# Loading halves of K, Q and V as pairs in an attention and token-mixing kernel

## The chip, the cores and the metric

The kernel runs on one core of one Trainium2 chip. The metric is the device time of one execution in microseconds (us). Five things work side by side: TensorE (PE, with its weight loads PEld), VectorE (DVE), ScalarE (ACT), GpSimd (POOL), and 16 DMA engines, for which in this kernel SyncE (SP) issues every transfer.

## The reference

Batch 8, 8 heads, sequence 576, head width 64. The first stage is a linear attention; the second mixes the tokens of each batch and ends in a 512 x 512 projection.

```python
r_q, r_k = maximum(q, 0), maximum(k, 0)          # per position: times cos and sin
q_p = concat(r_q * cos, r_q * sin); k_p = concat(r_k * cos, r_k * sin)
kv  = einsum('bhsf,bhsd->bhfd', k_p, v); z = sum(k_p, axis=s)
x   = (q_p @ kv) / (q_p @ z + 1e-6)              # heads side by side: [8, 576, 512]
W   = einsum('bsd,btd->bst', x @ w_q, x @ w_k) / 8
out = maximum(einsum('bst,btd->bsd', W, x), 0) @ w_out
```

The inputs q, k and v have 9.4 MB each in float32, the output has 9.4 MB.

## The kernel before

**Tiling.** The work of the first stage is cut into 16 half-batches H = 0 to 15: batch H // 2, four of its heads. A half-batch has two head pairs, called a (0) and b (1). A head pair of one input is 128 partitions x 576 float32, 288 KB, each partition one contiguous run of 2304 bytes. The text calls it a quarter, since four of them make one input of one batch. It lies in half of a buffer `raw[nm][H % 5]` (five buffers for each of k, q and v).

**The order is written out by hand.** `ORDER` is one long text of words, and a loop at the end (line 555 on) turns each word into instructions. Each engine has its own queue and does its words in the order in which they stand; across engines the framework sets semaphores where one instruction needs what another made. A word has a kind, a number, perhaps a or b for one head pair alone, `@A`, `@V` or `@G` for ACT, DVE or POOL, and `:n` for the bank of PSUM. The kinds that matter here:

- LQ, LK, LV: load quarters (line 145); LW0 to LW5: load w_q, w_k and four slices of w_out; ST: store one tile of the output (line 519). All go through SP's queue.
- RQ, RK: relu and cast of q, k (ACT line 203, else line 205). CV: cast of v (lines 209 to 213), VS: v times the table of cos and sin on DVE (line 234). VG: both in one on POOL, straight from the loaded v (line 248).
- QT, KV, N (lines 295 or 301, 275 or 285, 340): transposes of q, k-times-v sums, and numerators with denominators, on PE. QM, KE, EP, RC, X (line 393) evict and divide.
- XT or XR with XE, WK, WQ, KX, MX (line 489) with ME (lines 500, 502), WO (line 509) with OE (lines 209, 213): the second stage.

**SP's queue.** SP issues loads and stores in the order of the words. The framework gives the transfers eight semaphores in turn (DMAHW0 to DMAHW7), and a transfer waits until the one eight before it has landed. A load also waits until the engines have read what was in its buffer, five half-batches earlier; a store waits for its OE.

**Before the change** the words LQ0b and LQ0a, say, stand for two transfers; a word without a or b gave two transfers as well, by the loop in `load`.

Of the kernel before, what the change touches and what calls it, by code (L numbers as in the profile page):

```python
# [23 lines left out]


ORDER = """
LQ1a LV1b LQ1b LV1a LK1b LK1a LV0a LV0b LQ0b LQ0a LK0a LK0b LV3b LK3a LV3a LQ3b LQ3a LK3b LQ2a LW0
LV2a LV2b LW1 LK2a LQ2b LK2b TK TV CV1b@A TI T2 TZ CV1a@A TQ RQ1@G TB TW QT1:0 RK1b@V CV0@G LV5a
RQ0b@A VS1b RK1a@V VS1a KV1:6 KE1@A QM1 VS0 RQ0a@V RK0@A LK5a LV5b LK5b LQ5a LQ5b LQ4a LQ4b LV4a
LV4b LK4a LK4b RQ3a@A N2:2 N3:6 QT0:0 EP3@V EP2@V KV0:4 RJ1 X2 QM0 WU9:2 KE0@V VG3a WU6:0 N1:0 X3  # L30
EP1@V RQ3b@A N0:4 VG3b RK3@A XT1:2 RQ2a@G QT3:6 CV2a@G EP0@V RJ0 X1 XE1@A X0 QM3 KV3:0 XT0:4 KE3@A
N6:0 CW1@A EP6@A XE0@V VG2b LV7b LV7a CW0@A WK0:6 RC6 N7:2 WQ0:7 X6 RK2a@A VG5a KW0@A RQ5@G RQ2b@A
LQ7b LK7a LQ7a VS2a EP7@A RK2b@A LK7b LQ6a LQ6b LV6b LK6b LV6a LW4 LK6a LW2 LQ8b LW3 LV8a LW5 LV8b
LQ8a RC7 KX0:1 QW0@V QT2:4 X7 XK0@A KV2:0 XT3:2 RK5a@A KE2@A QM2 RK5b@A N5:6 N4:0 CV5b@V XA0@V VS5b
EP4@A EP5@A RC5 RQ4b@G RC4 KV5:4 X5 XE3@A MX0:2 X4 CV4a@G LV9a RQ4a@A LQ9a LQ9b LK8a XB0@G ME0@A
QT5:6 CV4b@G LV9b LK8b KE5@A XR2:2 QT4:0 MX2:4 QM5 N11:6 XE2@A ME2@A WK1:2 RK4a@G EP11@A KW1@A QM4
MX1:4 VS4 ME1@A RK4b@A LK9b LK9a N10:0 KX1:2 WQ1:3 CV7a@A KV4:4 EP10@V XK1@A RJ5 QW1@A XA1@A MX5:2
KE4@A VG7b X10 X11 ME5@A RQ7a@A MX4:0 VS7a ME4@A N9:6 RC9 XT5:4 RQ7b@G N8:2 XB1@V XE5@A RQ6@A X9
EP8@V RC8 RK7@G VG6b LV11b VG6a LV11a LQ11b LQ10b LQ11a LQ10a QT7:0 KV7:6 KE7@A X8 XT4:2 MX6:4 QM7
CW3@G CW2@G QT6:6 MX7:0 ME6@A XE4@V QM6 ME7@A N15:4 WK2:2 CV8a@G N14:0 MX3:6 RK6@A LK11b LK11a CW5@G  # L40
EP14@V EP15@V ME3@A WQ2:3 KV6:6 KW2@V RC14 RC15 VG8b KE6@A CW4@A QW2@V KX2:2 X14 N13:0 N12:6 X15
RK8a@G EP12@V XR7:4 WO8:3 XK2@A WO1:2 EP13@A XA2@A XE7@A WO7:5 OE8:0@A RQ8a@A OE1:4@A RJ6 VG9b X12
X13 WO2:4 RK9a@G RQ8b@A XR6:2 XB2@G CV9a@V MX8:0 OE2:2@A VS9a RQ9@A VS8a ME8@V OE7:1@A RK8b@A QT8:6
XE6@V RK9b@A WO6:4 QT9:0 QM8 WO4:3 OE6:3@A QM9 WK3:2 KW3@A KV8:6 KV9:4 MX9:0 OE4:5@A ST4 LV10b LV10a
LQ13b LQ12b LQ13a LK10a KE8@V MX11:2 N16:6 KE9@A ME11@A ME9@A WQ3:4 EP16@V KX3:5 MX10:2 RC16 X16
XK3@V QW3@A N19:0 VG11 ME10@A N18:6 EP18@V N17:4 WO11:2 RC17 EP19@A RK11b@G RC18 RC19 RK11a@G
RQ10a@G VG10 X19 WO5:3 RQ11@A X17 RQ10b@A OE11:6@A ST11 LQ12a LV12a LK10b LK12b LV13a LV12b LQ14b
LK12a LV15b LV13b LK13b LQ14a LK14a QT11:0 X18 WO9:2 XA3@A KV11:4 QT10:6 OE5:5@A OE9:7@A KE11@A QM11
XR8:2 RQ13@G XB3@A XE8@A XR9:0 WO10:4 WO0:5 QM10 N22:6 OE10:8@A EP22@A MX13:2 RQ12a@G RQ12b@G
OE0:6@A XE9@V ME13@V MX12:0 WO12:4 RC22 X22 ME12@A WK4:5 MX15:2 N23:0 KW4@A ME15@V EP23@A MX14:6  # L50
WQ4:5 KX4:2 ME14@A RC23 WO3:3 X23 RK10@A XK4@V XB4@V QW4@A XA4@A KV10:6 OE3:9@A QT13:0 QM13
OE12:10@A ST12 LV14a LK13a LV14b LK15a WO14:5 KE10@A VG12 MX16:2 XR11:6 XE11@V OE14:11@A ME16@A
RK12@A N20:0 N21:4 WO13:2 RC21 RC20 X21 QT12:6 MX18:4 X20 WO17:3 KV12:0 QM12 ME18@A MX19:4 OE13:10@A
ST13 LQ15b XR10:6 WO16:2 RQ14a@A KE12@A RQ14b@A ME19@A OE17:13@V ST17 LQ15a LK14b XE10@V VG13 MX17:6
N24:4 OE16:12@V N25:0 ME17@A RK13a@A RK13b@A QT14:2 EP24@V QM14 EP25@V WO21:7 WK5:6 RJ12 KW5@A
OE21:10@A ST21 LK15b ST8 ST3 LV15a KV13:2 KE13@A VG14 KX5:6 X24 X25 WQ5:7 N27:2 XR12:0 RK14a@A QW5@V
N26:4 EP27@V XE12@V XK5@A XB5@A WO20:6 EP26@A RK14b@A RJ13 XA5@G X27 RQ15b@G WO19:0 KV14:2 OE20:14@A
ST20 ST0 ST7 VG15b X26 MX23:6 OE19:15@A MX21:4 WO15:1 ME23@V KE14@A XR13:2 MX20:6 ME21@A VG15a
MX22:4 OE15:17@V XE13@V WO18:0 RQ15a@A N28:2 RK15b@A ME22@A ME20@A OE18:16@V ST18 ST16 ST14 ST10
ST19 ST15 N29:4 EP29@V EP28@V RK15a@A QT15:6 RJ14 WK6:0 X28 KW6@A WO25:1 KV15:2 WQ6:0 KE15@A X29  # L60
KX6:4 OE25:13@A ST25 ST6 ST2 ST5 ST1 QM15 XR14:2 N30:6 EP30@V RC30 QW6@A N31:0 XK6@A XE14@A WO23:4
X30 EP31@A RC31 XB6@V WO26:2 X31 OE23:12@A WO24:4 XR15:6 XA6@G OE26:10@V ST26 OE24:8@A MX27:2 MX24:0
ME27@A XE15@V WO22:5 WK7:2 ME24@A OE22:0@V ST22 ST23 ST9 ST24 KW7@A MX25:0 MX26:6 WQ7:4 KX7:2 ME25@A
XK7@A XA7@G ME26@V QW7@V XB7@A WO27:3 OE27:5@A ST27 WO29:2 MX28:0 ME28@A MX29:4 MX31:6 WO30:3
OE30:12@V ST30 ME29@A MX30:0 ME31@A WO28:4 ME30@A OE29:11@A ST29 WO32:5 WO33:2 OE32:9@A ST32
OE28:4@V ST28 OE33:8@V ST33 WO34:3 WO35:4 WO31:5 OE34:5@V ST34 OE35:0@V ST35 OE31:2@A ST31
"""


# [1 line left out]
def kernel(  # L71
# [10 lines left out]
    nc = tc.nc  # L82
# [18 lines left out]
    NRAW, NPREP, NV2, NQM, NX, NXT, NOUT = (5, 2, 2, 2, 2, 2, 18)  # L101
# [12 lines left out]
    def bufs(n, shape, dtype, name):  # L114
        return [pool.tile(shape, dtype, name=f"{name}{i}") for i in range(n)]

    raw = {nm: bufs(NRAW, [P, 2, HC], FP32, f"{nm}raw") for nm in "kqv"}
# [18 lines left out]
    def srcs(src):  # L136
        return [src[b].flatten().rearrange("(pr p e) -> p pr e", pr=NPAIR, p=P)
                for b in range(B)]

    src = {"k": srcs(k), "q": srcs(q), "v": srcs(v)}  # L140

    def load(nm, H, part):
        b, h = divmod(H, 2)
        for r in (0, 1) if part is None else (part,):
            nc.sync.dma_start(raw[nm][H % NRAW][:, r, :], src[nm][b][:, 2 * h + r, :])  # L145

    coef = math.pi / 2.0 / S
    ki = pool.tile([P, C, 2], I32, name="ki")
# [49 lines left out]
    A, V, G = nc.scalar, nc.vector, nc.gpsimd  # L198
# [356 lines left out]
    for word in ORDER.split():  # L555
        word, _, eng = word.partition("@")
        word, _, ps = word.partition(":")
        part = {"a": 0, "b": 1}.get(word[-1])
        word = word.rstrip("ab")
        kind = word[:2] if word[:2] in steps or word[:2] in halves or word[0] in "LT" else word[0]  # L560
        i, ps = int(word[len(kind):] or 0), int(ps or 0)
        if kind in ("LK", "LQ", "LV"):
            load(kind[1].lower(), i, part)
        elif kind in halves:
            halves[kind](i, ps, ENG.get(eng), slice(0, 2) if part is None else
                         slice(part, part + 1))
        else:
            steps[kind](i, ps, ENG.get(eng))
# [30 lines left out]
```

## Time and profile before

| | |
|---|---|
| time, median of 3 runs | 117.84 us (117.74 to 118.74) |
| profiled execution, its own time | 116.59 us |
| its span, first to last instruction | 114.8 us |
| TensorE clock granted | 0.996 |
| PE busy / PEld | 98.0 us / 65.9 us |
| DVE / ACT / POOL busy | 87.0 / 84.1 / 73.7 us |
| DMA packets on SP's queue | 20640, 39.07 MB, 93.0% of 16 engines' span |
| loads of q, k, v | 32 each, 288 KB, 5.8 to 5.9 us from issue to landing (median) |
| stores | 36, 256 KB, 3.6 us |

How to read it: times in the views of the trace count from the start of the span. The profiled execution's own time is 1.8 us more than its span, which is what lies before and after the program's instructions. A line with "x4" stands for four instructions in a row that are merged. A bracket at a row's end says how long the engine sat idle before it and what ended that. An issue on SP (SPq) is the instruction that starts a transfer, not the transfer.

### The profile page before, as it was taken

What the parts mean: (1) busy time and instruction counts of PE and PEld (TensorE: products, weight loads), DVE (VectorE), ACT (ScalarE), POOL (GpSimd) and SP (SyncE); (2) the same over time, 40 slices, a digit from 0 to 9 for tenths busy, and PEclk for the clock granted to TensorE, in tenths of its full rate; (3) what the DMA queues carried; (4) which work ended last, traced back from release to release, by engine and by line L of the source; (5) the groups of instructions that cost most, each with busy time, mean ns of one, the idle gap of its engine ahead of it and who ended that gap; (6) DMA issues with size and microseconds to landing.
All of it is one profiled execution on the core that took longest, in us unless ns stands there. A gap on an engine that the chain in (4) does not pass through costs nothing.

```text
span 114.8 us, 4994 instructions
## 1 busy us (share of the span) xinstructions
PE 98.0 (85%) x2126; PEld 65.9 (57%) x2126; DVE 87.0 (76%) x159; ACT 84.1 (73%) x154; POOL 73.7 (64%) x62
## 2 busy tenths in 40 slices
PE   0034897897988998999999999999999999999970
PEld 0034666785776876646875566655774666563420
DVE  2039997899899998799679967798887896751450
ACT  7553419588999986999799959969678849568520
POOL 7434069965889799959699994999999901010000
PEclk9999999999999999999999999999999999999998
DMA  3999999999999999999999999999879579886494
GB/s 105 308 361 407 398 388 333 384 388 391 390 391 389 391 390 389 390 394 388 386 394 400 383 380 369 393 329 328 292 258 335 202 266 371 336 338 257 186 373 175
DMA packets 20662, 39.38 MB, mean 343 GB/s; under 512 B 3232, under 2 KB 3232, under 8 KB 20640
## 3 DMA queue, kind: packets, MB, share of 16 engines
q1 hardware_dynamic: 20640, 39.07, 93.0%
q8 instruction: 16, 0.26, 1.0%
q14 instruction: 6, 0.05, 0.1%
HBM read 29.62 MB, written 9.44 MB: 340 GB/s over the span
## 4 chain that ended last, share of the span: by engine, by line
PE 55%; DMA 16%; DVE 11%; ACT 6%; POOL 6%; SPq 2%; issue 2%; POOLq 0%; ACTq 0%; DVEq 0%
PE ps L509 26%; DMA vraw<-in_v_dram 10%; DMA wkf<-in_moe_w_k_dram 6%; PE ps L340 6%; PE ps L285 5%; POOL v L248 4%; DVE x L393 4%; PE ps L439 3%; PE ps L489 3%; PE ps L466 3%; PE ps L452 3%; PE ps L419 2%; SPq L145 2%; DVE v L234 1%; PE ps L295 1%
## 5 line engine op out<-in xcount | busy, mean ns | idle before, releaser
L248 POOL TENSOR_TENSOR v<-vraw,vtab 128x1152 bf16<-128x1152 f32 (+1 forms) x16 | 49.6, 3111 | 9.3 <-DMA vraw<-in_v_dram 5.6
L509 PE MATMUL ps<-wow,mix 128*128 128x512 bf16 x144 | 34.9, 380 | 0.0
L393 DVE TENSOR_TENSOR x<-ps,rec 128x640 bf16<-128x640 f32 x32 | 25.3, 820 | 0.7
L509 PEld LDWEIGHTS <-mix 128*128 128x128 bf16 x144 | 12.4, 98 | 14.1 <-issue 1.6
L209 ACT COPY o<-ps 128x512 f32<-128x512 f32 x25 | 14.6, 588 | 5.9 <-PE ps L509 5.4
L500 ACT ACTIVATE mix<-ps 128x576 bf16<-128x576 f32 x27 | 16.9, 651 | 1.8 <-PE ps L489 1.8
L203 ACT ACTIVATE rk<-kraw 128x576 bf16<-128x576 f32 (+1 forms) x18 | 14.4, 814 | 1.9 <-DMA kraw<-in_k_dram 1.8
L316 DVE TENSOR_TENSOR qm<-ps,qtab 128x1152 bf16<-128x1152 bf16 x22 | 15.4, 748 | 0.3 <-PE ps L295 0.3
L340 PE MATMUL ps<-kvs,qm 64*128 64x65 bf16 x640 | 14.7, 196 | 0.9 <-ACT kvs L209 0.8
L340 PEld LDWEIGHTS <-qm 64*128 64x128 bf16 x640 | 13.0, 98 | 3.8 <-issue 2.9
L295 PE MATMUL ps<-ident,rq 128*128 128x128 bf16 x99 | 8.3, 236 | 7.8 <-POOL rq L205 7.3
L203 ACT ACTIVATE rq<-qraw 128x576 bf16<-128x576 f32 (+1 forms) x15 | 11.5, 784 | 4.7 <-DMA qraw<-in_q_dram 4.6
L213 DVE COPY o<-ps 128x512 f32<-128x512 f32 x11 | 7.6, 689 | 6.2 <-ACT mix L500 3.3
L285 PE MATMUL ps<-v,rk 64*64 64x130 bf16 x432 | 9.9, 234 | 2.5 <-DVE v L234 1.4
L295 PEld LDWEIGHTS <-rq 128*128 128x128 bf16 x99 | 6.6, 106 | 9.2 <-POOL rq L205 7.6
L205 POOL TENSOR_SCALAR rq<-qraw 128x576 bf16<-128x576 f32 (+1 forms) x10 | 8.5, 860 | 3.9 <-DMA qraw<-in_q_dram 3.4
L285 PEld LDWEIGHTS <-rk 64*64 64x64 bf16 x432 | 7.9, 115 | 5.5 <-issue 1.0
L211 POOL TENSOR_SCALAR kx<-kx 64x256 bf16<-64x256 bf16 x5 | 2.0, 402 | 11.1 <-ACT kx L209 10.8
L209 ACT CAST kvs<-ps 128x260 bf16<-128x260 f32 (+1 forms) x14 | 6.2, 441 | 4.0 <-PE ps L285 3.7
L489 PE MATMUL ps<-wq,kx 64*128 64x288 bf16 x64 | 8.1, 287 | 0.4 <-POOL kx L211 0.3
L234 DVE TENSOR_TENSOR v<-vb,vtab 128x1152 bf16<-128x1152 bf16 (+1 forms) x9 | 8.4, 937 | 0.1
L209 ACT COPY xT<-ps 128x1280 bf16<-128x1280 bf16 (+1 forms) x7 | 8.2, 1178 | 0.1
(66 smaller groups left out, 132.3 us busy)
## 6 DMA issues: line engine op xcount, KB each, us to landing
qraw<-in_q_dram SPq DMA_DIRECT2D x32, 288.0 KB, 5.9
vraw<-in_v_dram SPq DMA_DIRECT2D x32, 288.0 KB, 5.8
kraw<-in_k_dram SPq DMA_DIRECT2D x32, 288.0 KB, 5.9
out_dram<-o SPq DMA_DIRECT2D x36, 256.0 KB, 3.6
wof<-in_moe_w_out_dram SPq DMA_DIRECT2D x4, 256.0 KB, 6.0
wqf<-in_moe_w_q_dram SPq DMA_DIRECT2D x1, 128.0 KB, 6.8
wkf<-in_moe_w_k_dram SPq DMA_DIRECT2D x1, 128.0 KB, 6.6
```

What stands on the lines that cost most here:

```text
L203: A.activation(dst, s, AF.Relu)
L209: A.copy(dst, s)
L234: V.tensor_mul(v2_b[H % NV2][:, part, :, :, 0:D], vb_b[H % NPREP][:, part].unsqueeze(3).to_broadcast([P, n, C, 2, D]), vtab.unsqueeze(1).t ...
L248: G.tensor_mul(dst[:, part, :, :, 0:D], s[:, part].unsqueeze(3).to_broadcast([P, n, C, 2, D]), vtab.unsqueeze(1).to_broadcast([P, n, C, 2, ...
L285: nc.tensor.matmul(kv_v[o, r, :], rk_of(H)[a, pr, c, :], v2_b[H % NV2][a, pr, c, :, 0:D + 1], start=(c == 0), stop=(c == C - 1))
L295: nc.tensor.transpose(qt_v[:, c, :], rq_b[H % NPREP][:, c, :, :], ident)
L316: V.tensor_mul(qm_b[H % NQM][:, :, r, 0:C, :], q_t[:, r].unsqueeze(1).to_broadcast([P, 2, C, H2]), qtab)
L340: nc.tensor.matmul(nv[:, pr, u, :], qm_b[H % NQM][a, s, r, 2 * u:2 * u + 2, :], kv_b[H % 2][a, r, pr if H in KV_WIDE else 0, s, 0:D + 1], ...
L393: V.tensor_tensor(x_b[b % NX][:, :, 4 * h:4 * h + 4, :].rearrange("p u (w r) d -> p r w u d", r=2)[:, r], nv[:, :, :, 0:D], rec(g).to_broa ...
L489: nc.tensor.matmul(pair(ps)[:, t, :].bitcast(FP32)[:, 0:HS], kx_b[b % 2][a, (m // 2) ^ t, (m % 2) * P:(m % 2 + 1) * P], wq_b[b % 2][a, :], ...
L500: A.activation(dst, s, AF.Relu, scale=scale_moe)
L509: nc.tensor.matmul(o, mix_b[bp % 2][:, m, rt * P:(rt + 1) * P], wow[:, m, :], start=(m == 0), stop=(m == NDM - 1))
```

## The change

Twenty-three pairs of words become one word each, and `load` makes of such a word one transfer of 128 x 2 x 576 float32 (576 KB) in place of two. In the DRAM the two runs of a partition lie 288 KB apart, in the buffer side by side. Where the two words of a pair did not stand next to each other, one was moved. Beside that some other words change places: LW0 goes behind LV2b, LW5 ahead of LV8a, LQ12b ahead of LQ13, LV15a from behind ST3 to ahead of LK13a; CW2 goes ahead of CW3 on POOL, WK2 ahead of N15 on PE, and RK11b and RK11a become one instruction on POOL.

```diff
 LQ1a LV1b LQ1b LV1a LK1b LK1a
-LV0a LV0b LQ0b LQ0a LK0a LK0b LV3b LK3a LV3a LQ3b LQ3a LK3b LQ2a LW0 LV2a LV2b LW1 LK2a
+LV0 LQ0b LQ0a LK0 LV3b LV3a LQ3b LQ3a LK3 LQ2a LV2a LV2b LW0 LW1 LK2a
...
     def load(nm, H, part):
         b, h = divmod(H, 2)
-        for r in (0, 1) if part is None else (part,):
-            nc.sync.dma_start(raw[nm][H % NRAW][:, r, :], src[nm][b][:, 2 * h + r, :])
+        r = slice(0, 2) if part is None else slice(part, part + 1)
+        nc.sync.dma_start(raw[nm][H % NRAW][:, r, :],
+                          src[nm][b][:, 2 * h + r.start:2 * h + r.stop, :])
```

The pairs, in the order of the words: LV0, LK0, LK3, LQ5, LK4, LV7, LQ7, LK7, LQ6, LK6, LQ8, LQ9, LV11, LQ11, LQ10, LK11, LV10, LQ13, LK12, LV12, LQ14, LV13, LV14.

Three places in the queues. First SP, from the loads of half-batch 4 to those of 6. The name ends in the number of the buffer and a number of the framework: kraw4 holds k of half-batch 4, vraw2, qraw2 and kraw2 hold half-batch 7, qraw1, vraw1 and kraw1 half-batch 6. Before:

```order
L145 DMA kraw4_67<-in_k_dram 128x576 x2
L145 DMA vraw2_75<-in_v_dram 128x576 x2
L145 DMA qraw2_70<-in_q_dram 128x576
L145 DMA kraw2_65<-in_k_dram 128x576
L145 DMA qraw2_70<-in_q_dram 128x576
L145 DMA kraw2_65<-in_k_dram 128x576
L145 DMA qraw1_69<-in_q_dram 128x576 x2
L145 DMA vraw1_74<-in_v_dram 128x576
L145 DMA kraw1_64<-in_k_dram 128x576
L145 DMA vraw1_74<-in_v_dram 128x576
L527 DMA wof_133<-in_moe_w_out_dram 128x512
L145 DMA kraw1_64<-in_k_dram 128x576
```

The same place after the change:

```order
L144 DMA kraw4_67<-in_k_dram 128x2x576
L144 DMA vraw2_75<-in_v_dram 128x2x576
L144 DMA qraw2_70<-in_q_dram 128x2x576
L144 DMA kraw2_65<-in_k_dram 128x2x576
L144 DMA qraw1_69<-in_q_dram 128x2x576
L144 DMA vraw1_74<-in_v_dram 128x576 x2
L527 DMA wof_133<-in_moe_w_out_dram 128x512
L144 DMA kraw1_64<-in_k_dram 128x2x576
```

Fourteen transfers became nine. LQ7a now comes ahead of LK7a, and LK6b behind LV6a and LW4. The bytes ahead of LV6b (the first vraw1) are the same.

Second, SP between the stores ST12 and ST13 (both from buffer o10): vraw4 is v of half-batch 14, kraw3 k of 13, kraw0 k of 15, vraw0 v of 15. One piece of the difference:

```order
-L145 DMA vraw4_77<-in_v_dram 128x576
-L145 DMA kraw3_66<-in_k_dram 128x576
-L145 DMA vraw4_77<-in_v_dram 128x576
-L145 DMA kraw0_63<-in_k_dram 128x576
+L144 DMA vraw0_73<-in_v_dram 128x576
+L144 DMA kraw3_66<-in_k_dram 128x576
+L144 DMA vraw4_77<-in_v_dram 128x2x576
+L144 DMA kraw0_63<-in_k_dram 128x576
```

LV15a came in ahead of LK13a, and LV14 is whole and stands where its second half stood.

Third, POOL at the relu of k of half-batch 11 (buffer kraw1 to rk1), the one place where POOL's rows differ (the exchange of CW2 and CW3 does not show, since both read and write the same tile):

```order
 L248 TENSOR_TENSOR v21_85<-vraw1_74,vtab_127 128x36x64
-L205 TENSOR_SCALAR rk1_79<-kraw1_64 128x576 x2
+L205 TENSOR_SCALAR rk1_79<-kraw1_64 128x1152
 L205 TENSOR_SCALAR rq0_80<-qraw0_68 128x9x64
 L248 TENSOR_TENSOR v20_84<-vraw0_73,vtab_127 128x36x64
```

Two instructions became one of twice the width; nothing else moved there.

More of the change, by code (lines that the diff above doesn't have):

```diff
@@ L26 @@
 ORDER = """
[L27 to L66, printed above, removed]
+LQ1a LV1b LQ1b LV1a LK1b LK1a LV0 LQ0b LQ0a LK0 LV3b LV3a LQ3b LQ3a LK3 LQ2a LV2a LV2b LW0 LW1 LK2a
@@ new lines @@
+LQ2b LK2b TK TV CV1b@A TI T2 TZ CV1a@A TQ RQ1@G TB TW QT1:0 RK1b@V CV0@G LV5a RQ0b@A VS1b RK1a@V
+VS1a KV1:6 KE1@A QM1 VS0 RQ0a@V RK0@A LK5a LV5b LK5b LQ5 LQ4a LQ4b LV4a LV4b LK4 RQ3a@A N2:2 N3:6
+QT0:0 EP3@V EP2@V KV0:4 RJ1 X2 QM0 WU9:2 KE0@V VG3a WU6:0 N1:0 X3 EP1@V RQ3b@A N0:4 VG3b RK3@A XT1:2
+RQ2a@G QT3:6 CV2a@G EP0@V RJ0 X1 XE1@A X0 QM3 KV3:0 XT0:4 KE3@A N6:0 CW1@A EP6@A XE0@V VG2b LV7
+CW0@A WK0:6 RC6 N7:2 WQ0:7 X6 RK2a@A VG5a KW0@A RQ5@G RQ2b@A LQ7 VS2a EP7@A RK2b@A LK7 LQ6 LV6b LV6a
+LW4 LK6 LW2 LW3 LW5 LV8a LV8b LQ8 RC7 KX0:1 QW0@V QT2:4 X7 XK0@A KV2:0 XT3:2 RK5a@A KE2@A QM2 RK5b@A
@@ new lines @@
+N5:6 N4:0 CV5b@V XA0@V VS5b EP4@A EP5@A RC5 RQ4b@G RC4 KV5:4 X5 XE3@A MX0:2 X4 CV4a@G LV9a RQ4a@A
+LQ9 LK8a XB0@G ME0@A QT5:6 CV4b@G LV9b LK8b KE5@A XR2:2 QT4:0 MX2:4 QM5 N11:6 XE2@A ME2@A WK1:2
+RK4a@G EP11@A KW1@A QM4 MX1:4 VS4 ME1@A RK4b@A LK9b LK9a N10:0 KX1:2 WQ1:3 CV7a@A KV4:4 EP10@V XK1@A
+RJ5 QW1@A XA1@A MX5:2 KE4@A VG7b X10 X11 ME5@A RQ7a@A MX4:0 VS7a ME4@A N9:6 RC9 XT5:4 RQ7b@G N8:2
+XB1@V XE5@A RQ6@A X9 EP8@V RC8 RK7@G VG6b VG6a LV11 LQ11 LQ10 QT7:0 KV7:6 KE7@A X8 XT4:2 CW2@G MX6:4
+QM7 CW3@G QT6:6 MX7:0 ME6@A XE4@V WK2:2 QM6 ME7@A N15:4 CV8a@G N14:0 MX3:6 RK6@A LK11 CW5@G WQ2:3
@@ new lines @@
+EP14@V EP15@V ME3@A KV6:6 KW2@V RC14 RC15 VG8b KE6@A CW4@A QW2@V KX2:2 X14 N13:0 N12:6 X15 RK8a@G
+EP12@V XR7:4 WO8:3 XK2@A WO1:2 EP13@A XA2@A XE7@A WO7:5 OE8:0@A RQ8a@A OE1:4@A RJ6 VG9b X12 X13
+WO2:4 RK9a@G RQ8b@A XR6:2 XB2@G CV9a@V MX8:0 OE2:2@A VS9a RQ9@A VS8a ME8@V OE7:1@A RK8b@A QT8:6
+XE6@V RK9b@A WO6:4 QT9:0 QM8 WO4:3 OE6:3@A QM9 WK3:2 KW3@A KV8:6 KV9:4 MX9:0 OE4:5@A ST4 LV10 LQ12b
+LQ13 LK10a KE8@V MX11:2 N16:6 KE9@A ME11@A ME9@A WQ3:4 EP16@V KX3:5 MX10:2 RC16 X16 XK3@V QW3@A
+N19:0 VG11 ME10@A N18:6 EP18@V N17:4 WO11:2 RC17 EP19@A RC18 RC19 RK11@G RQ10a@G VG10 X19 WO5:3
@@ new lines @@
+RQ11@A X17 RQ10b@A OE11:6@A ST11 LQ12a LK10b LK12 LV12 LQ14 LV13 LV15b LK13b LK14a QT11:0 X18 WO9:2
+XA3@A KV11:4 QT10:6 OE5:5@A OE9:7@A KE11@A QM11 XR8:2 RQ13@G XB3@A XE8@A XR9:0 WO10:4 WO0:5 QM10
+N22:6 OE10:8@A EP22@A MX13:2 RQ12a@G RQ12b@G OE0:6@A XE9@V ME13@V MX12:0 WO12:4 RC22 X22 ME12@A
+WK4:5 MX15:2 N23:0 KW4@A ME15@V EP23@A MX14:6 WQ4:5 KX4:2 ME14@A RC23 WO3:3 X23 RK10@A XK4@V XB4@V
+QW4@A XA4@A KV10:6 OE3:9@A QT13:0 QM13 OE12:10@A ST12 LV15a LK13a LV14 LK15a WO14:5 KE10@A VG12
+MX16:2 XR11:6 XE11@V OE14:11@A ME16@A RK12@A N20:0 N21:4 WO13:2 RC21 RC20 X21 QT12:6 MX18:4 X20
@@ new lines @@
+WO17:3 KV12:0 QM12 ME18@A MX19:4 OE13:10@A ST13 LQ15b XR10:6 WO16:2 RQ14a@A KE12@A RQ14b@A ME19@A
+OE17:13@V ST17 LQ15a LK14b XE10@V VG13 MX17:6 N24:4 OE16:12@V N25:0 ME17@A RK13a@A RK13b@A QT14:2
+EP24@V QM14 EP25@V WO21:7 WK5:6 RJ12 KW5@A OE21:10@A ST21 LK15b ST8 ST3 KV13:2 KE13@A VG14 KX5:6 X24
+X25 WQ5:7 N27:2 XR12:0 RK14a@A QW5@V N26:4 EP27@V XE12@V XK5@A XB5@A WO20:6 EP26@A RK14b@A RJ13
+XA5@G X27 RQ15b@G WO19:0 KV14:2 OE20:14@A ST20 ST0 ST7 VG15b X26 MX23:6 OE19:15@A MX21:4 WO15:1
+ME23@V KE14@A XR13:2 MX20:6 ME21@A VG15a MX22:4 OE15:17@V XE13@V WO18:0 RQ15a@A N28:2 RK15b@A ME22@A
@@ new lines @@
+ME20@A OE18:16@V ST18 ST16 ST14 ST10 ST19 ST15 N29:4 EP29@V EP28@V RK15a@A QT15:6 RJ14 WK6:0 X28
+KW6@A WO25:1 KV15:2 WQ6:0 KE15@A X29 KX6:4 OE25:13@A ST25 ST6 ST2 ST5 ST1 QM15 XR14:2 N30:6 EP30@V
+RC30 QW6@A N31:0 XK6@A XE14@A WO23:4 X30 EP31@A RC31 XB6@V WO26:2 X31 OE23:12@A WO24:4 XR15:6 XA6@G
+OE26:10@V ST26 OE24:8@A MX27:2 MX24:0 ME27@A XE15@V WO22:5 WK7:2 ME24@A OE22:0@V ST22 ST23 ST9 ST24
+KW7@A MX25:0 MX26:6 WQ7:4 KX7:2 ME25@A XK7@A XA7@G ME26@V QW7@V XB7@A WO27:3 OE27:5@A ST27 WO29:2
+MX28:0 ME28@A MX29:4 MX31:6 WO30:3 OE30:12@V ST30 ME29@A MX30:0 ME31@A WO28:4 ME30@A OE29:11@A ST29
@@ L67 @@
+WO32:5 WO33:2 OE32:9@A ST32 OE28:4@V ST28 OE33:8@V ST33 WO34:3 WO35:4 WO31:5 OE34:5@V ST34 OE35:0@V
+ST35 OE31:2@A ST31
 """
```

## The prediction

> **What bounds the kernel now.** I read the slices of the page first, then the stages, then the chain of waits, then the queues around the place where the chain changes its engine. The slices (40 of 2.87 us each) of PE and of the DMA engines:
>
> ```profile
> PE   0034897897988998999999999999999999999970
> DMA  3999999999999999999999999999879579886494
> GB/s 105 308 361 407 398 388 333 384 388 391 390 391 389 391 390 389 390 394 388 386 394 400 383 380 369 393 329 328 292 258 335 202 266 371 336 338 257 186 373 175
> ```
>
> From the second slice to the 26th or so the DMA engines are full, at 388 to 394 GB/s in most slices; from the 17th on PE is full. Where one takes over from the other is seen in two stages (busy us by engine, then clock, DMA share, GB/s):
>
> ```profile
> 8.00:45.20 37.20, 31.66 (x727) 25.25 (x727) 34.62 (x66) 27.95 (x48) 26.23 (x18) 1.00 1.06 387
> 45.20:111.20 66.00, 65.69 (x1399) 40.02 (x1398) 51.18 (x88) 50.94 (x98) 42.88 (x26) 1.00 0.92 337
> ```
>
> In the 66.00 us after 45.20 PE is busy for 65.69: it has 0.31 us to give back. Before that it sits idle for 5.54 of 37.20 us. The chain (start, us, what) says what holds it there:
>
> ```profile
> 9.13 5.99 DMA vraw<-in_v_dram
> 15.13 0.02 issue
> 15.14 6.64 DMA wkf<-in_moe_w_k_dram
> ...
> 40.42 4.71 POOL v L248 x2
> 45.13 0.04 issue
> 45.17 0.72 PE ps L285 x36
> ...
> 105.82 5.30 PE ps L509 x24
> ```
>
> First loads, then evictions, then POOL's two VG instructions of half-batch 6, then at 45.17 the 36 matmuls of KV6, and from there on nearly nothing but PE. So the end is the start of KV6 plus about 66 us of PE work plus the 3.6 us of last store. **Only what moves KV6, or makes PE wait after it, moves the time.**
>
> The middle rows also show how SP works: a load issued at 9.13 landed at 15.13, and at 15.14 the transfer eight places behind it went out. In the full stretch an issue therefore tells, less 0.02, when the transfer eight before it landed. The issues on SP (start, us, how long the issue took):
>
> ```profile
> 33.10 0.33 SPq L145 DMA_DIRECT2D qraw<-in_q_dram  x1
> 33.86 0.33 SPq L145 DMA_DIRECT2D vraw<-in_v_dram  x1
> 34.59 0.33 SPq L145 DMA_DIRECT2D kraw<-in_k_dram  x1
> 35.35 0.33 SPq L145 DMA_DIRECT2D vraw<-in_v_dram  x1
> ...
> 40.26 0.33 SPq L145 DMA_DIRECT2D vraw<-in_v_dram  x1
> ```
>
> These are LQ6b, LV6b, LK6b, LV6a and LV8a, so LK4b landed at 33.08, LV7b at 33.84, LV7a at 34.57, LQ7b at 35.33 and LV6b at 40.24. A quarter lands every 0.75 us. POOL and DVE at that place:
>
> ```profile
> 33.02 0.67 POOL L205 TENSOR_SCALAR rk<-kraw 128x576 bf16<-128x576 f32 x1
> 34.00 3.12 POOL L248 TENSOR_TENSOR v<-vraw,vtab 128x1152 bf16<-128x1152 f32 x1 [0.32 <-DMA vraw<-in_v_dram]
> 37.10 1.17 POOL L205 TENSOR_SCALAR rq<-qraw 128x576 bf16<-128x576 f32 x1
> 38.23 1.15 POOL L205 TENSOR_SCALAR rk<-kraw 128x1152 bf16<-128x1152 f32 x1
> 40.40 4.71 POOL L248 TENSOR_TENSOR v<-vraw,vtab 128x1152 bf16<-128x1152 f32 x2 [1.02 <-DVE x L393]
> 33.44 1.45 DVE L234 TENSOR_TENSOR v<-vb,vtab 128x2304 bf16<-128x2304 bf16 x1
> 36.86 0.88 DVE L234 TENSOR_TENSOR v<-vb,vtab 128x1152 bf16<-128x1152 bf16 x1
> ```
>
> They are RK4a, VG7b, RQ7b, RK7, then VG6b with VG6a; on DVE VS4 and VS7a. VG7b starts 0.16 after its load landed, and so does VG6b (40.24 to 40.40; the DVE instruction named in its bracket writes x, which VG6b does not read, and ends at 40.41, so I take the load). KV6 thus hangs on the landing of LV6b: plus 0.16, plus 4.71, is 45.11. If that came earlier, ACT's ME3 is next, since it empties the bank for KV6:
>
> ```profile
> 43.20 1.16 ACT L203 ACTIVATE rk<-kraw 128x1152 bf16<-128x1152 f32 x1
> 44.27 0.63 ACT L500 ACTIVATE mix<-ps 128x576 bf16<-128x576 f32 x1
> ```
>
> It ends at 44.90, so KV6 can gain about 0.2 us before something else is late.
>
> **The change part by part.** *Fewer transfers.* The bytes ahead of LV6b are the same; nine pairs (LV0 to LQ6) stand ahead of it. What a boundary between two transfers costs the engines no row shows. From above: a quarter at 390 GB/s takes 0.756 us, at 407, the best full slice, 0.725, so at most 0.03. From below: nothing. The GB/s row does not fall in slices 13 to 16 (389 to 391), where the shorter transfers of w_out bring more boundaries, so I take 0.01. Nine times that is **-0.09 us** on KV6, bounds 0 and -0.27, the latter cut to -0.2 by ME3.
>
> *A first half waits for its second.* In a pair the second half lands when it did, the first one quarter or more later. Sixteen of the 23 are read by one instruction already, which waited for both: nothing. Of the seven others, LQ8, LQ10, LQ14 and LK11 are read behind KV6, where PE sets the pace; with LQ8 and LQ14 the half that is read first landed second in any case. LQ7 stands one place earlier, so lands near 36.0, against 37.10 for RQ7b: nothing. Two remain. RK4a now waits for LK4b, 33.08 + 0.16 = 33.24 in place of 33.02: +0.2, and VS4 behind it on DVE as much. VG7b waits for LV7a: 34.57 less 0.06 for six boundaries, plus 0.16, is 34.67 in place of 34.00: +0.67. Queued behind it on POOL are RQ7b and RK7; PE waits for them with QT7 and KV7:
>
> ```profile
> 39.02 0.66 PE L295 MATMUL ps<-ident,rq 128*128 128x128 bf16 x9
> 39.61 1.19 PE L275 MATMUL ps<-v,rk 64*128 64x260 bf16 x18
> 45.17 0.72 PE L285 MATMUL ps<-v,rk 64*64 64x130 bf16 x36 [0.38 <-POOL v L248]
> ```
>
> If all 0.67 went through, RK7 would end at 40.05 in place of 39.38 and KV7 start some 0.48 late. PE idles 0.38 before KV6, of which 0.22 are free of ME3 (44.95 against 45.17), so KV6 would be 0.26 late. But VG7b took 3.12 where each of VG6 took 2.36: 0.76 were lost, and VS4 ran until 34.89. RQ7b took 1.17 against 0.67 for RK4a, and VS7a ran until 37.74. Twice an instruction on POOL that began under a VS ended as if it had begun 0.14 before that VS ended (37.12 - 2.36 = 34.76; 38.27 - 0.67 = 37.60). By these rows the 0.67 fall into a time that VG7b loses anyway, and only the 0.2 by which RK4a pushes VS4 are left: RK7 ends near 39.6, KV7 starts at 39.6. **0 us**, bounds 0 and +0.26.
>
> The Trainium skill, SBUF — State Buffer, section "Who interferes with whom", says so as a rule: DVE with two inputs in SBUF and a POOL instruction that reads SBUF take a shared port in turns, and the later one is blocked altogether. By it the sum is 0 here; were it a slowdown that travels with the instruction, it would be +0.26. The trace agrees with the rule, with the two differences above.
>
> VG6b itself is not reached: RK7 ends at 39.4 to 40.05, VG6b waits for its load until 40.3.
>
> *Exchanges.* LV3a, LQ3b, LQ3a and LV2 land 0.7 earlier, but ACT's CW1 still waits for wkf, with the same bytes ahead of it: 0. LW0 lands 1.5 later, before wkf: 0. LK6b moves behind LV6a; RK6 waits for LK6a, as before, and ACT has no idle time before it (its row at 43.20 has no bracket): 0. WK2 goes ahead of N15 on PE, to 42.43, and needs XE4 from DVE:
>
> ```profile
> 41.65 0.75 DVE L213 COPY xT<-ps 128x1152 bf16<-128x1152 bf16 x1
> 42.43 0.49 PE L340 MATMUL ps<-kvs,qm 64*128 64x65 bf16 x20
> ```
>
> XE4 ends at 42.40, just in time: 0; should it come 0.2 late with VS4, PE waits 0.2, which the 0.22 before ME3 cover. RK11 whole takes 1.15 (as RK7) for two of 0.67 on POOL, which does not hold the chain by then: 0.
>
> *Late loads.* LV15a comes forward past ST13, ST17, ST21, ST8 and ST3, and LV14 lands up to a quarter later. The rows:
>
> ```profile
> 72.01 13.65 POOL L248 TENSOR_TENSOR v<-vraw,vtab 128x2304 bf16<-128x2304 f32 x3 [1.83 <-PE ps L285]
> 86.86 4.80 POOL L248 TENSOR_TENSOR v<-vraw,vtab 128x1152 bf16<-128x1152 f32 x2
> 74.06 1.41 SPq L145 DMA_DIRECT2D vraw<-in_v_dram  x1
> DMA to landing us min/median/max: 3.3/5.8/6.9
> ```
>
> The first row is VG12, VG13 and VG14 without a gap to 85.66, so VG14 begins at 81.1. LV14b went out at 74.06; with the median of 5.8 it lands at 79.9, a quarter later at 80.6: covered. With the longest, 6.9, it would land at 81.7, 0.6 late. VG15a (half of the second row) ran right behind VG15b, so that loading it earlier gains nothing. 0, bounds 0 and +0.6.
>
> *SP.* 23 issues of 0.33 to 0.43 go, 8 to 10 us of SP's time. SP spends the full stretch waiting for semaphores, and with eight transfers in flight that now hold more bytes, the engines run dry no sooner: 0. A store behind SP's waits has 18 output buffers as cover.
>
> **Sum:** -0.09. Against the profiled execution 116.59 becomes 116.50; that execution ran 1.25 below the median of the three, so on the median 117.84 becomes **117.75**.
>
> **The rivals.**
>
> *A pair flows faster.* For it: per-transfer work halves. Against: the flat GB/s row. At the best slice's rate, 18 quarters ahead of LV6b save 18 x 0.03 = 0.56; ACT and PE come along only in part (the 0.2 above if not). 117.3 to 117.6. The Trainium skill, DMA: Bandwidth & Descriptors, section "Rules for kernel authors", tells to coalesce into transfers of 1 MiB or more, and its "Anatomy of one DMA" puts about 2.0 us of fixed cost on each (fitted there on POOL's path). By that estimate nine fewer would save 18 us if they ran one after the other. The trace disagrees: a quarter lands every 0.75 us with eight under way.
>
> *A pair flows slower.* Its source has two runs for each partition. The nearest row is the slice with w_q, whose transfer has four runs for each: 333 GB/s against 390, 15% (its runs are nine times shorter). Price at the row's 15%: 9 pairs x 1.51 x 0.15 = 2.0 us at LV6b, hence 119.8; it passes 1% (1.18 us) from 9% on. At half the row: +1.0, 118.8.
>
> *POOL is late at LV7:* KV7 and KV6 late by up to 0.26, 118.0 to 118.1.
>
> *It does not do what it says:* the engines still move runs of 2304 bytes, and nothing else about them changes: 117.84.
>
> **How the numbers follow.** Forecast, with the case of no effect, 117.6 to 117.9: 0.73. POOL late: 0.08. Faster flow: 0.06. Slower flow: 0.08, of which 0.05 beyond 1%. For what the trace cannot show, half to each side: 0.05. The three runs before spread to 118.74 and the profiled one lay at 116.59, so the range takes in some of that, with the bounds +0.26 and +0.6: 117.1 to 118.5. About 1% is what a measurement of this kernel can tell from no change. Faster by over 1% (under 116.66) has no case of its own beyond half of the unseen and the far end of a faster flow: 0.05. Slower by over 1% (over 119.02): 0.08. Within: 0.87.
>
> **What would show it.** LV6b landing at 40.1 to 40.2 and KV6 at 45.0 to 45.2; VG7b starting near 34.7 yet ending at 37.1 to 37.4, so taking about 2.6; KV7 at 39.6; GB/s still 388 to 394 in the full slices; 368 fewer packets on SP's queue (23 x 16); PE busy for 65.5 or more of the 66 us from KV6 on. Wrong if KV6 moves by over 0.3, if a new idle time of PE over 0.3 stands behind it, or if the GB/s row shifts by 2%.

## The result, and the profile after

Over 22 runs each, the changed kernel takes 118.16 us in the median (before: 117.48); its time is **1.0095 of before, 95% interval 1.0067 to 1.0123**, about 1.1 us more. A second set of runs gave 1.0118 (1.0066 to 1.0170). I had forecast no change. Some executions of each kernel, before among them, are disturbed and longer; the ratios leave them out, and a profile that fell into one (the first of the split kernel, the one without warm-up, the second of before) is not read for times.

The profiled execution of the change ran 117.49 us with a span of 115.7 (before 116.59 and 114.8). Much is where I put it. The page of the change, its GB/s slices and its queues:

```profile
GB/s 99 299 357 408 394 392 331 381 391 390 389 394 390 388 390 391 395 388 390 388 401 366 339 363 400 396 288 385 355 149 349 195 264 377 380 275 260 184 375 169
q1 hardware_dynamic: 20272, 39.07, 92.4%
q8 instruction: 16, 0.26, 1.0%
```

The full slices still run at 388 to 395 GB/s, and there are 368 packets fewer on SP's queue. POOL's timeline (start, us, engine, line, what), and the chain of waits of the change:

```profile
33.49 0.67 POOL L205 TENSOR_SCALAR rk<-kraw 128x576 bf16<-128x576 f32 x1 [0.30 <-DMA kraw<-in_k_dram]
35.02 2.58 POOL L248 TENSOR_TENSOR v<-vraw,vtab 128x1152 bf16<-128x1152 f32 x1 [0.86 <-DMA vraw<-in_v_dram]
40.51 2.38 POOL L248 TENSOR_TENSOR v<-vraw,vtab 128x1152 bf16<-128x1152 f32 x1 [0.66 <-DMA vraw<-in_v_dram]
```

```profile
30.38 9.97 DMA vraw<-in_v_dram
40.34 0.03 issue
...
40.51 4.73 POOL v L248 x2
45.24 0.04 issue
45.28 0.72 PE ps L285 x35
...
55.19 1.17 PE ps L285 x68
56.36 1.09 issue
57.45 0.21 PE ps L285
57.66 0.35 PE ps L489 x4
```

VG7b waits for the whole of LV7 and takes 2.58 us, LV6b still sets VG6b, and KV6 starts at 45.28 against 45.17. What is new stands near the end of the chain: PE does the first 35 matmuls of KV9, stands still for 1.09 us, and does the last one. "Issue" means that PE waited for nothing that the profile shows: no semaphore, no data. In before the same place reads:

```profile
55.07 1.17 PE ps L285 x60
56.24 0.09 issue
56.33 0.21 PE ps L285
```

The stages of before, then of the change, cut at KV6 and at that stand (us, PE busy, then the other engines):

```profile
45.17:56.33 11.16, 11.07 (x261) 7.35 (x261) 10.26 (x17) 9.77 (x18) 9.22 (x9) 1.00 1.05 390
56.33:111.12 54.79, 54.64 (x1138) 32.70 (x1137) 40.96 (x71) 41.12 (x79) 33.66 (x17) 1.00 0.89 327
```

```profile
45.28:57.45 12.17, 11.08 (x262) 7.36 (x262) 10.47 (x18) 9.77 (x18) 9.16 (x9) 1.00 1.05 390
57.45:111.99 54.54, 54.52 (x1138) 32.72 (x1137) 40.98 (x71) 41.15 (x79) 33.44 (x16) 1.00 0.88 321
```

PE's work in the first stage is the same (11.07 and 11.08), the stage is 1.01 us longer. With KV6 0.11 later and the rest 0.25 shorter, that makes +0.87, the 0.9 by which the span grew. In these two profiles one stand of PE is the whole difference.

**What PE waits for there.** Beside SP's queue the page lists "q8 instruction", 16 packets, 0.26 MB: 16 blocks of 16 KB. PE has 2126 weight loads and 2126 matmuls; 16 blocks spread over them are about 256 instructions or 128 pairs each. I call the matmul at which a new block begins an edge. The single packets of that queue lie 4 to 7 us apart, each but the last over 2 us ahead of a matmul whose number is 988 plus or minus a multiple of 128, and the stand is at the matmul numbered 988 (counted from 0) in both kernels. So I took the 16 packets for **PE's own instructions, fetched during the run**: in the first 90 us of the run a fetch begins some time after PE has passed the edge before, its packet takes 0.9 to 1.2 us while the DMA engines are full, and PE can go on about 1.2 us later. In us, worked out from single packets of the trace:

```
edge at matmul           PE passes the    fetch for edge   packet   plus    PE runs
                         edge before      starts           took     1.22    matmul 988
988, kernel before       51.22            53.98 (+2.75)    1.14     56.34   56.33
988, changed kernel      51.34            55.06 (+3.72)    1.16     57.43   57.45
```

From the edge at 860 to the one at 988 PE needs 5.0 us, the shortest stretch while the DMA engines are full (the others there: 5.8 to 6.5). In before the fetch was ready just in time. In the change it starts 0.97 us later, and PE stands. At the other edges up to 63 us it is still ready 0.3 to 1.0 us early (before: 0.4 to 2.1).

### The profile page after: what moved, and what is told of

Read it like the earlier page. It is cut to its first block, busy times and chain, and to the rows that moved or that the text cites. A ratio compares the mean times of both kernels' runs of the same rounds, so it can differ in the third digit from the quotient of the medians.

```text
span 115.7 us, 4966 instructions
## 1 busy us (share of the span) xinstructions
PE 97.5 (84%) x2126; PEld 65.4 (57%) x2126; DVE 86.7 (75%) x159; ACT 84.2 (73%) x154; POOL 72.8 (63%) x61
## 4 chain that ended last, share of the span: by engine, by line
PE 57%; DMA 32%; POOL 4%; SPq 2%; issue 1%; ACT 1%; POOLq 0%
PE ps L509 29%; DMA qraw<-in_q_dram 18%; DMA vraw<-in_v_dram 9%; PE ps L340 5%; PE ps L285 5%; DMA kraw<-in_k_dram 5%; POOL v L248 4%; PE ps L489 4%; PE ps L466 3%; PE ps L419 3%; PE ps L439 3%; PE ps L452 3%; SPq L144 2%; PE ps L301 1%; PE ps L295 1%
## 5 line engine op out<-in xcount | busy, mean ns | idle before, releaser
L248 POOL TENSOR_TENSOR v<-vraw,vtab 128x1152 bf16<-128x1152 f32 (+1 forms) x16 | 49.0, 3076 | 9.9 <-PE ps L285 3.9
```

Source lines behind the costliest of these rows:

```text
L248: G.tensor_mul(dst[:, part, :, :, 0:D], s[:, part].unsqueeze(3).to_broadcast([P, n, C, 2, D]), vtab.unsqueeze(1).to_broadcast([P, n, C, 2, ...
```

## The experiments

Theory A: the joined transfers hold up PE's instruction fetch. Rival B: the moved and exchanged words do it. Later a split of A: A1, the size of one transfer; A2, the bytes in flight.

**1. Size or order.** The order of the change, quarters again:

```diff
-        r = slice(0, 2) if part is None else slice(part, part + 1)
-        nc.sync.dma_start(raw[nm][H % NRAW][:, r, :],
-                          src[nm][b][:, 2 * h + r.start:2 * h + r.stop, :])
+        for r in (0, 1) if part is None else (part,):
+            nc.sync.dma_start(raw[nm][H % NRAW][:, r, :], src[nm][b][:, 2 * h + r, :])
```

> The changed kernel with its own order of the work, but each of the 23 joined words issues its two 288 KB quarters again, one behind the other (the moves and exchanges stay, the transfer size goes back). Theory A, the size of the transfers holds up PE's own instruction fetch: the 1.09 us stand of PE at the last matmul of KV9 shrinks to 0.3 us or less, and the ratio to the kernel before is 0.997 to 1.003. Theory B, the exchanges and the moved loads are the cause: the stand stays at about 1.1 us and the ratio near 1.009.

Measured 0.9976 (0.9946 to 1.0005). The timeline of PE:

```profile
56.72 0.21 PE L284 MATMUL ps<-v,rk 64*64 64x130 bf16 x1 [0.29 <-issue]
```

The same kernel once more, later:

> The changed order with every pair as two quarters, once more: lead of the fetch 2.6 to 3.0 us, stand 0.1 to 0.4 us, ratio 0.995 to 1.001 as in the first experiment.

1.0005 (0.9968 to 1.0042); this time all 72 matmuls of KV8 and KV9 run through:

```profile
54.73 1.25 PE L284 MATMUL ps<-v,rk 64*64 64x130 bf16 x72
```

B falls: with every word where the change puts it the loss is gone. It is the joining alone.

**2. Does the stand come again?** The changed kernel again:

> The changed kernel once more, beside the other three on the same chip, for a second profile of it. Theory A: the stand at KV9's last matmul is there again, 0.8 to 1.2 us, with the fetch 3.4 to 3.8 us behind the edge; ratio 1.007 to 1.012. If the stand was an accident of one profiled execution: no stand, and the ratio has to come from elsewhere.

1.0118 (1.0066 to 1.0170), fetch 3.67 us behind the edge, and on PE's timeline:

```profile
57.25 0.21 PE L285 MATMUL ps<-v,rk 64*64 64x130 bf16 x1 [1.25 <-issue]
```

Here KV6 started at 44.93, 0.24 earlier than in before, and the kernel was still slower.

**3. Which pairs.** Four loads are in flight when the fetch is due: LV11, LQ11, LQ10, LK11. Before, with these four alone joined (and the reverse: the change with these four split):

```diff
-VG6b LV11b VG6a LV11a LQ11b LQ10b LQ11a LQ10a QT7:0
+VG6b VG6a LV11 LQ11 LQ10 QT7:0
...
-RK6@A LK11b LK11a
+RK6@A LK11
```

> The kernel before, with nothing changed but four loads, the second to last of those in flight ahead of KV9: LV11, LQ11, LQ10 and LK11 become one transfer of 576 KB each. Theory A in its local form (what is in flight while the instructions of that one stretch are fetched): PE stands 0.9 to 1.2 us at the last matmul of KV9, and the ratio is 1.006 to 1.010. Theory B: no stand beyond the 0.1 us of before, ratio 0.998 to 1.002. If A holds but the whole row of pairs is needed for it, the ratio lies at 1.000 as well, and the stretches fetched earlier show leads no longer than in before.

> The changed kernel, with LV11, LQ11, LQ10 and LK11 alone as two quarters each again; the other 19 pairs stay. Theory A in its local form: PE's stand at the last matmul of KV9 falls from 1.09 us to 0.3 us or less, and the ratio to the kernel before is 0.998 to 1.003. Theory B, or A only with the whole row of pairs: the stand stays above 0.8 us, ratio 1.007 to 1.010.

> The changed kernel with LV11, LQ11, LQ10 and LK11 alone as quarters, for a second profile. With about 1,700 KB in flight at the edge as in the kernel before, the fetch starts 2.7 to 3.1 us behind it, PE stands 0.1 to 0.5 us at the last matmul of KV9, and the ratio is 0.997 to 1.003. If the pairs elsewhere matter, the stand is above 0.8 us and the ratio 1.006 to 1.011.

Joined alone: 0.9994 (0.9955 to 1.0032). Split alone: 0.9989 (0.9952 to 1.0027), and, run again, 1.0006 (0.9977 to 1.0036). PE's timelines, four joined, then four split:

```profile
56.97 0.21 PE L286 MATMUL ps<-v,rk 64*64 64x130 bf16 x1 [0.61 <-issue]
```

```profile
56.97 0.21 PE L285 MATMUL ps<-v,rk 64*64 64x130 bf16 x1 [0.59 <-issue]
```

Either half leaves a stand of 0.6 us, between the two kernels. So the four near pairs are half of it, and neither local form of A holds in full. A stand 0.5 us longer than before's would be 0.4% of the time. The ratios do not show it, though their upper ends are only 0.3 to 0.4% above before. With one profile a kernel, I can't say how the stand varies from execution to execution, so how much of the time each part of the stand costs stays open.

**4. Is it the instructions?** No load is touched here; small matmuls, whose results nothing uses, move PE's block edges through the program:

```diff
+    def FI(i, ps, eng):
+        for _ in range(i):
+            nc.tensor.matmul(bank(ps)[0:H2, 0:H2], wc[0:H2, 0:H2], wc[0:H2, 0:H2], start=True, stop=True)
...
-RQ1@G TB TW
+RQ1@G TB FI32:2 TW
```

With 32 of them in before:

> The kernel before, no load touched, with 32 small 64x64 matmuls more (their results are not used) behind the word TB, where PE waits for its first data anyway. If PE's instructions come in blocks of 128 pairs of weight load and matmul, the edges fall 32 matmuls earlier in the program's work, two of them into the shortest stretches of time. Theory A, worked out with the leads of the kernel before: PE stands about 0.8 us near 47.4 us and about 0.7 us near 59.5 us, and perhaps 0.3 us near 85; ratio 1.010 to 1.016. Any theory in which the stand comes from the changed loads alone, or in which PE's own instructions play no part: nothing but the small matmuls in the ramp, ratio 0.998 to 1.004.

1.0300 (1.0243 to 1.0357), and on PE's timeline, in the middle of a run of transposes:

```profile
46.65 0.39 PE L419 MATMUL ps<-ident,x 64*128 64x64 bf16 x15
48.99 0.24 PE L419 MATMUL ps<-ident,x 64*128 64x64 bf16 x5 [1.95 <-issue]
```

That is matmul 860, which is 988 less 128: an edge, 32 places earlier in the program than before's edge there. Quarters alone, the old order, and PE stands for 1.95 us, because this stretch lasts only 3.7 us of PE work. The stand is longer than my 0.8, since the fetch came 3.23 us behind its edge where I had taken 2.2 from one profile; it also left none for 59.5. The ratio is a miss: 3% where I had 1.0 to 1.6. Beside the stand PE waits later for other engines, 0.46 us before 80.29, 0.72 before 82.26 and 0.57 before 96.63, behind a store that lands late and a late load of v; that I had not foreseen. The place of the stand shows that PE waits for its own instructions.

With 16 in the changed kernel (`FI16:2` at the same place):

> The changed kernel with 16 small 64x64 matmuls more (their results are not used), put on PE just behind the word TB, where PE waits for data anyway; no load is touched. If PE's instructions come in blocks of 128 pairs of weight load and matmul (theory A), each block's edge now falls 16 matmuls earlier in the program's work: the stand at the last matmul of KV9 is gone, and one of 0.5 to 1.0 us stands instead about 4 us later, near 60.5 us; ratio 1.004 to 1.010. If the stand belongs to KV9, its data or its place (any theory but A), it stays at KV9's last matmul with 1.1 us.

1.0170 (1.0101 to 1.0238), above my forecast. The 72 matmuls of KV8 and KV9 stay in one row:

```profile
56.07 1.53 PE L285 MATMUL ps<-v,rk 64*64 64x130 bf16 x72
```

The stand has left KV9's last matmul, as A says; 0.08 us of it are left at 57.16, at matmul 988 by count, 16 places earlier in the program. The one that I expected at 60.5 did not come (few bytes were in flight then, and the fetch began 1.1 us behind its edge); smaller ones without any releaser did, 0.25 up to 50.96 and 0.41 up to 88.72, at matmuls 860 and 1755 by count, the one an edge, the other one place off. These do not add up to the 1.9 us that its profiled run is above before's: KV6 is 0.65 later as well, and why stays open.

The changed kernel without its three warm-up matmuls, which moves the edges the other way by three:

```diff
-X2 QM0 WU9:2 KE0@V VG3a WU6:0 N1:0
+X2 QM0 KE0@V VG3a N1:0
```

> The changed kernel, no load touched, without the three warm-up matmuls WU9 and WU6 (their results are not used; PE waits for N1's data there either way). The edges of PE's instruction blocks then fall three matmuls later: the edge that stood at KV9's last matmul falls into WK4's or MX9's longer work behind it. Theory A: the stand of 1.09 us is gone or below 0.3 us, though every pair of loads is still one transfer; ratio to the kernel before 0.998 to 1.004. Any theory in which the pairs or the exchanges cost by their data, their landing or the memory they share: the stand and the ratio of 1.009 stay.

1.0141 (1.0100 to 1.0183): a miss in time. I had worked it out with times of the changed kernel that held the stand itself; without it the new stretch is no longer than the old one. Its profile is read for the place alone, and the place is telling:

```profile
56.32 0.64 PE L285 MATMUL ps<-v,rk 64*64 64x130 bf16 x32
56.88 0.30 PE L489 MATMUL ps<-wq,kx 64*128 64x288 bf16 x2
58.17 0.30 PE L489 MATMUL ps<-wq,kx 64*128 64x288 bf16 x2 [0.98 <-ACT kvs L209]
```

KV9 now ends without a stand, and PE stands behind MX9, at the first matmul of MX11, again matmul 988 by count, three places later in the program. (The bracket names ACT, which by the trace had released it at 57.39; PE went on at 58.17.) Four more stands without a releaser follow, up to 70.01, 76.20, 81.09 and 86.07, at matmuls 1244, 1372, 1500 and 1627 by count: three edges, and one place off a fourth. Stands keep to the edges even where they come at other times.

**5. Size of a transfer, or bytes in flight.** SP keeps eight transfers in flight. Transfers of 32 bytes into a tile that nothing reads take some of the eight places, so that fewer bytes are in flight at unchanged transfer sizes:

```diff
+    junk = pool.tile([P, 128], FP32, name="junk")
+
+    def JD(i, ps, eng):
+        nc.sync.dma_start(junk[0:1, 8 * i:8 * i + 8], src["q"][0][0:1, 0, 0:8])
...
-LV11 LQ11 LQ10 QT7:0
+LV11 JD2 LQ11 JD3 LQ10 JD4 QT7:0
```

Five of them in the changed kernel (two more behind LQ8 and LQ9):

> The changed kernel with five more transfers of 32 bytes (into a tile that nothing reads), one behind each of LQ8, LQ9, LV11, LQ11 and LQ10, so that with eight transfers in flight as ever, only about as many bytes are in flight while KV8 and KV9 run as in the kernel before, each pair still being 576 KB. A1, the size of one transfer holds up the fetch: it starts 3.4 to 3.8 us behind the edge before it as in the changed kernel, stand 0.8 to 1.1 us, ratio 1.007 to 1.011. A2, the bytes in flight hold it up: 2.7 to 3.0 us, stand 0.3 us or less, ratio 0.998 to 1.003.

1.0023 (0.9992 to 1.0053), beside 1.0118 for the plain change on the same chip. All 23 pairs are still 576 KB, the fetch starts 2.91 us behind the edge, and the stand is half as long:

```profile
57.00 0.21 PE L285 MATMUL ps<-v,rk 64*64 64x130 bf16 x1 [0.58 <-issue]
```

So A2, if not down to 0.3. More of them, in the changed kernel (15), in before (11) and in the quartered one (7):

> The changed kernel, every pair still one transfer of 576 KB, with 15 transfers of 32 bytes (into a tile that nothing reads) among the loads from LQ8 to LQ10: two behind each pair and one behind each quarter, so that of eight transfers in flight only three or so carry a load. If the bytes in flight set how long PE's fetch waits, the wait falls further than with five of them (2.91 us behind the edge, stand 0.58 us): 1.5 to 2.5 us, stand 0.1 us or less, ratio 0.995 to 1.001. If a pair's size sets it, 2.9 us or more and a stand of 0.5 us or more remain, ratio 1.002 to 1.008.

> The kernel before, with eleven transfers of 32 bytes among its quarter loads from LQ9a to LK11b, nothing else. If the bytes in flight set the wait of PE's fetch, the fetch for the edge in KV9 starts less than 2.5 us behind the edge before it (2.75 in before), PE's stand of 0.1 us there is gone, and the kernel runs at 0.996 to 1.000 of before. If they don't, or the loads themselves become late by the smaller depth, 1.000 to 1.006.

> The changed kernel's order with every pair as two quarters again, as in the first experiment (0.998 of before, stand 0.29 us), and seven transfers of 32 bytes among them from LQ9 to LQ10. By the bytes in flight: fetch less than 2.7 us behind the edge, stand 0.1 us or less, 0.994 to 0.999 of before, which would be the fastest of all. Otherwise as the first experiment, 0.996 to 1.001.

1.0355 (1.0319 to 1.0390), 1.0389 (1.0343 to 1.0434) and 1.0217 (1.0163 to 1.0271). No stand is left at KV9's last matmul in any, and all are slower, far above my forecasts, since loads now come late. The first of them, PE and POOL:

```profile
65.31 0.49 PE L285 MATMUL ps<-v,rk 64*64 64x130 bf16 x20 [1.60 <-POOL rk L205]
```

```profile
64.11 1.15 POOL L205 TENSOR_SCALAR rk<-kraw 128x1152 bf16<-128x1152 f32 x1 [1.86 <-DMA kraw<-in_k_dram]
```

Each small transfer takes its turn among the eight, so the loads behind it start later. Four of them, right ahead of the fetch, in the quartered order and in before, and beside them before itself:

> The changed order with quarters and four transfers of 32 bytes, one behind each of LK9b, LK9a, LV11 and LQ11. By the bytes in flight (about 1,200 to 1,450 KB at the edge instead of 1,737): lead 1.8 to 2.5 us, no stand, no load late, 0.994 to 0.999 of before. If a smaller depth makes loads late at once, 1.003 or more.

> The kernel before with four transfers of 32 bytes, one behind each of LK9a, LV11b, LV11a and LQ11b. By the bytes in flight (about 1,200 to 1,450 KB at the edge instead of 1,723): lead 1.8 to 2.5 us, no stand, 0.996 to 1.000 of before. If a smaller depth makes loads late at once, 1.003 or more.

> The kernel before once more, for a second profile. If its single profile is typical: the fetch for the edge in KV9 2.6 to 2.9 us behind the edge before it, stand 0.0 to 0.2 us, ratio 0.998 to 1.002. If the stand of before varies as widely as that of the half-undone kernels, 0.3 to 0.6 us, then only some half of the 1% is the stand.

The first: 1.0117 (1.0058 to 1.0176); no stand in KV9, but 0.92 us at KV11, where RK11 waits for LK11, whose second quarter landed at 61.69 (before: 59.94):

```profile
63.07 0.72 PE L284 MATMUL ps<-v,rk 64*64 64x130 bf16 x36 [0.92 <-POOL rk L204]
```

The second has no ratio (118.36 us in the profiled run, 120.64 in the median of six) and the same kind of wait, 0.91 us. Before against itself is 0.998 (0.9934 to 1.0026); in its second profile, too, the 72 matmuls of KV8 and KV9 run through. No version here beats before.

All profiles that are read and have their edges where before has them, by the bytes that were issued but not yet moved when PE passed the edge at 860 (worked out from SP's issues and the packets; counted by the packets' recorded ends, each figure is 125 to 156 KB lower, in the same order):

```
kernel                               KB in flight   fetch starts   PE stands   ratio to
                                     at the edge    after it, us   us          before
quarters + 7 small transfers              567           0.35          0        1.0217
change + 15 small                         791           1.16          0        1.0355
before + 11 small                         823           1.02          0        1.0389
before + 4 small                         1108           0.94          0        -
quarters + 4 small                       1174           1.48          0        1.0117
quarters, second profile                 1508           2.23          0        1.0005
change + 5 small                         1581           2.91          0.58     1.0023
change, four pairs split                 1677           2.86          0.59     1.0006
before                                   1723           2.75          0.09     1
quarters                                 1737           2.88          0.29     0.9976
before, four pairs joined                2839           3.13          0.61     0.9994
change, second profile                   2873           3.67          1.25     1.0118
change                                   2902           3.72          1.09     1.0095
```

At this edge the fetch's wait follows the bytes in flight, from 0.35 us at 567 KB to 3.7 at 2900. Kernels with quarters and kernels with pairs lie on one line (1581 KB in pairs and 1723 in quarters: 2.91 and 2.75). It is no plain queue: the 1179 KB by which the change exceeds before take 3.1 us at 390 GB/s, and the fetch comes 0.97 us later. Nor is it a law for every edge. Counted by the packets' ends, before has 1431 KB in flight when PE passes the edge at 476 and the change 2520, and the fetches start 3.11 and 3.22 us behind it; in before the edge at 732 has 1538 KB, and the fetch starts 1.88 us behind it. So the bytes in flight are shown as the cause for the edge around which they were varied, and not beyond it. What else stays open: why four joined pairs alone, with 2839 KB, wait 3.13 and not 3.7; and why at 2.75 to 2.91 the stand is anything from 0.09 to 0.59: there PE went on 1.2 to 1.5 us behind the packet's end.

## Why the prediction was wrong

- **The failed step** is in the paragraph on SP: "with eight transfers in flight that now hold more bytes, the engines run dry no sooner: 0." I saw that the bytes in flight would rise and asked only whether the engines could run dry. I did not ask who else waits behind those bytes. PE's instructions do, and that is +1.0 us in the profile, 1.1 by the ratio.
- **"Only what moves KV6, or makes PE wait after it, moves the time"** held to the letter. But for "makes PE wait" I looked at data alone. The row "q8 instruction" stood on the page of before, and so did the 0.09 "issue" in its chain at KV9; I read neither. The check that I had named, PE's idle time from KV6 on, is what failed: 1.11 us in the change (66.71 less 65.60, from the stages above) where before has 0.24.
- **Fewer transfers, -0.09:** cannot be told. KV6 starts at 45.28 and 44.93 in two profiles of the change, at 45.17, 45.36 and 44.89 in profiles with quarters. The flat GB/s row, on which the term rested, was right, so neither rival on the flow came. (The first listing of SP's queue ahead of the prediction has fifteen transfers, not fourteen, that became nine; the nine pairs counted here stay.)
- **A first half waits for its second, 0 us:** right in kind. VG7b took 2.58 (forecast 2.6); VS4 ended at 35.37, and 35.37 - 0.14 + 2.36 is 37.59, where VG7b ended at 37.60. It started at 35.02 and not 34.7, because the loads ran 0.3 late there (LK4 landed at 33.35), and KV7 came at 39.91, not 39.6; KV6 waited for LV6b all the same (0.66 idle on POOL ahead of it).
- **Exchanges, late loads, 0 us:** right. The order alone is 0.9976 and 1.0005 of before.
- **The rivals:** none was the one that came. "POOL is late at LV7" names nearly the measured median, by another way. That the median, 118.16, lies inside my range of 117.1 to 118.5 is luck as well: no term of the range stood for this wait. The chance for "slower by over 1%" was too small for a change that raises what is in flight by two thirds (1723 to 2902 KB).

## What to carry to other kernels

A transfer costs not only its own landing: here PE's own instructions, which come in during the run, came later when more bytes were in flight, and a program of two thousand short matmuls waits for them. When the profile shows PE standing with "issue" and no semaphore, count its matmuls from the last such place; if the distance is a multiple of 128, or one off, look at when that stretch began and what was in flight. With a fixed number of transfers in flight, joining them raises the depth; here too much depth held up the fetch, and too little made the loads late (four to fifteen small transfers among them; only the five in the changed kernel cost nothing), so size and depth are one choice.

## What the hardware showed

PE's instructions come in during the run: 16 packets of 16 KB, one for each 256 instructions, which the page counts among the packets of the 16 DMA engines. The Trainium skill, Trainium Architecture — The Big Picture, section "The software stack", gives an instruction 64 bytes, which agrees (16 KB / 256). The same section says that the streams are brought to each engine when the program is loaded; here 16 blocks came while it ran, and 32 idle matmuls more moved a stand of 1.95 us to a new place.

A fetch does not get its turn at once. At the edge in KV9 it starts 0.35 us behind the edge before with 567 KB of loads in flight and 3.7 us with 2900. The Trainium skill, DMA: Bandwidth & Descriptors, section "Queues, rings and completion order", has each engine take turns between queues after one packet of some 9 to 17 descriptors. A quarter lands every 0.75 us, so by that rule I would estimate that the fetch is held up for one transfer: 0.75 us behind quarters, 1.5 behind pairs. The runs do not bear that out, as far as they can tell: it started 2.2 to 2.9 us behind the edge at about 1500 to 1740 KB in flight, in quarters or in pairs. When a fetch is asked for no row shows, so part of that time may lie ahead of the queue.
